# Spreading the narrowing of feed-forward weights over the routed experts and over single operations

## The chip, the cores and the metric

The kernel runs on one core of one Trainium2 chip. The metric is the time of one execution on the device, in microseconds (us). TensorE is called PE, VectorE DVE, ScalarE ACT, GpSimd POOL, and SyncE, which issues most transfers, SP.

## The reference, cut to what matters

```python
def reference(**kwargs):
    attn_out = _attn_ref(q, k, v)              # decayed linear attention, 4 x 8 heads x 768 x 64
    x = tokens_by_512(attn_out)                # 3072 tokens x 512
    x = _moe_ref(x, ...)                       # 8 experts, one per token (argmax): relu(x @ w1[e]) @ w2[e], gated
    return _moe2_ref(x, ...)                   # dense: rms norm, then silu(xn @ w_gate) * (xn @ w_val) @ w_out
```

The first feed-forward layer is routed: each token uses one of 8 experts (512 to 1024 to 512). The second is dense: 512 to 1536, gated, and back to 512. Its three matrices make 36 tiles of 128 x 512.

## The kernel before

The kernel has three stages: attention with the routing (up to about 173 us of the profile), the eight routed experts one after the other (w = 0 to 7, largest first, with 448 down to 368 tokens each), and the dense layer over 8 blocks of 384 tokens, taken in four passes of two blocks each. Only the first pass (p == 0) has to prepare weights; the other three reuse them.

**High and low parts.** The matmuls run on rounded 32-bit floats, so each operand is split in a high part and a rest, and a product is three matmuls. `split_weights` (L178) makes the two parts of a weight tile: ACT copies it to the high part (L179), POOL subtracts (L180). An expert has 8 tiles of 128 x 1024 (64 in all, numbered t = 8 w + f). Activations are split by ACT and DVE: after `up` (12 matmuls, L285) ACT writes `hh` (L291) and DVE `hl` (L292); `down` (12 matmuls, L298) uses `hh` in eight matmuls and `hl` in the last four. In the loop, `up` of tile t comes before `down` of tile t-1.

**Narrowing.** The dense layer's weights arrive as 64-bit numbers. `uconvs_to` (L209) turns a tile into floats: ACT works on the high words twice (L219, L220), DVE takes four operations (L223, L226, L229, L232), and `umove` (L206) then splits the result, one tile late, with ACT (L179) and POOL (L180). Two tiles share one weight slot, and the results pass through two buffers `fu`. The 36 tiles are called u0 to u35.

**Slots and order.** There are 12 weight slots of 128 x 2 x 1024 (`NSLOT`), three raw buffers for arriving tiles (`NRAW`), and each engine works through its own queue in the order in which the program is written. Expert tile t uses slot t % 12, and its conversion is written up to nine steps ahead of its use (`convs_to`, L829 on). Dense tiles take the slots that come free behind the experts, 7 of them narrowed during the last expert (one for each step from t = 57 on), 7 more up to the first two feed-forward slices, and then three in each slice f of the first pass: one whole tile between the two blocks' `gate`s and two whole tiles after the second.

**The dense layer's slice.** `gate` (L740) makes 24 matmuls (L747) for one block and slice, then ACT takes the silu (L754), DVE multiplies (L755), ACT rounds (L756) and DVE subtracts (L757); `project` (L761) makes 9 matmuls with the result (L765). Both blocks write the same two banks `ps[:, 0]` and `ps[:, 1]`. While an expert runs, `settle` normalises the one before it on DVE: squares are added (L326), halved (L334), inverted (L343) and the rows scaled (L347).

Of the kernel before, what the change touches and what calls it, by code (L numbers as in the profile page):

```python
# [103 lines left out]
def fused_kernel(  # L104
# [60 lines left out]
    def wslot(t):  # L165
        return wt[t % NSLOT if t < NWT + NSLOT else t - NWT]

# [16 lines left out]

    state = {"load": 0, "conv": 0, "end": NPRE, "uload": 0, "uconv": 0}

    def loads_to(t):
        while state["load"] < min(t, state["end"]):
            n = state["load"]
            load_expert_weights(raw[n % NRAW], window_expert(n // NF), n % NF)  # L190
            state["load"] += 1

    def convs_to(t):
        while state["conv"] < min(t, state["end"]):
            n = state["conv"]
            loads_to(n + NRAW - 1)
            split_weights(wslot(n), raw[n % NRAW])
            state["conv"] += 1

    def uraw(u):  # L200
        return raw[(NWT + u) % NRAW].bitcast(I32)

    def uloads_to(u):
        while state["uload"] < min(u, NU):
            SP.dma_start(out=uraw(state["uload"]), in_=wm2[state["uload"]].bitcast(I32))
            state["uload"] += 1  # L206

    def umove(j):
        split_weights(wslot(NWT + j // 2), fl_u[j % 2], j % 2)  # L209

    def uconvs_to(n):
        n = min(n, NU)
        while state["uconv"] < n:
            j = state["uconv"]
            uloads_to(j + NRAW)
            v = uraw(j).rearrange("p (c t) -> p c t", t=2)
            lo, hi = v[:, :, 0], v[:, :, 1]
            u, b = fl_u[j % 2], fl_b[0]
            ACT.activation(out=u, in_=hi, func=AF.Abs, scale=2.0 ** -20)  # L219
            ACT.activation(out=u, in_=u, func=AF.Abs, bias=mid)  # L220
            if j:
                umove(j - 1)
# [3 lines left out]
            DVE.scalar_tensor_tensor(  # L226
                out=b, in0=lo, scalar=29, in1=b, op0=ALU.logical_shift_right, op1=ALU.bitwise_or
            )
            DVE.scalar_tensor_tensor(  # L229
                out=b, in0=hi, scalar=-(1 << 30), in1=b, op0=ALU.bitwise_and, op1=ALU.bitwise_or  # L230
            )
            DVE.scalar_tensor_tensor(out=u, in0=u, scalar=127.0, in1=b.bitcast(F32), op0=ALU.is_le, op1=ALU.mult)  # L232
            state["uconv"] += 1
            if j == NU - 1:
                umove(j)

# [179 lines left out]
    with ExitStack() as es:  # L416
# [289 lines left out]
        totals_b()  # L706
        state["end"] = NWT

# [165 lines left out]
    gate(1, 0)  # L874
    uconvs_to(8)
    project(0, 0)
    ex.mean(w, n, 3)
    ex.store(w - 1, CAPS[w - 1], wpos(w - 1), both(w - 1))
    gate(0, 1)
    uconvs_to(9)  # L880
    ex.inverse(0, n // 2)
    project(1, 0)
    gate(1, 1)
    uconvs_to(11)
    ex.inverse(n // 2, n)
    project(0, 1)
    gate(0, 2)
    uconvs_to(12)
    project(1, 1)
    gate(1, 2)  # L890
    uconvs_to(13)
# [3 lines left out]
    uconvs_to(14)  # L895
# [74 lines left out]
    with tc.If(flag > 0):  # L970
# [33 lines left out]
        with ExitStack() as es:  # L1004
            staging(es)
            wc = pool(es, "wcb")
            wt.extend(wc.tile([128, 2, 1024], F32R, name=f"wb{i}") for i in range(NSLOT, NW2))
            state.update(uload=0, uconv=0)
            uconvs_to(NU)
# [57 lines left out]
```

## Time and profile before

| what | us |
|---|---|
| median of 3 runs (lowest, highest) | 1119.85 (1118.16, 1119.85) |
| the profiled execution's own time | 1119.29 |
| its span in the profile | 1117.2 |
| PE busy | 1055.5 (94%) |
| DVE, ACT, POOL busy | 550.9, 381.4, 337.2 |

The span is the time between the first and the last instruction of the program; about 2.1 us of the execution lie outside it. The busy time of PE counts a matmul from its start to its modelled end, and matmuls overlap, so short pauses vanish in it. The routed experts run from about 173 to 490 us, the first pass of the dense layer from about 490 to 655 us, and the other three passes after that.

### The profile page before, as it was taken

How to read it: one execution, taken by the hardware profiler on the slowest of the kernel's cores; microseconds unless marked ns; L12 is line 12 of the kernel's file. 1: busy time of each engine (PE TensorE's matmuls, PEld its weight loads, DVE VectorE, ACT ScalarE, POOL GpSimd, SP SyncE). 2: the span in 40 equal slices, each digit the busy share in tenths (PEclk: the TensorE clock that was granted, in tenths of full speed). 3: DMA queues.
4: the chain of work that ended last, by engine and by line, in shares of the span. 5: the costliest groups of instructions: out<-in, count | busy, mean ns of one | idle time of the engine just before them, and what ended most of it. 6: DMA issues, size and time to landing. Idle time of an engine off the chain costs nothing.

```text
span 1117.2 us, 16379 instructions
## 1 busy us (share of the span) xinstructions
PE 1055.5 (94%) x6393; PEld 982.8 (88%) x6394; DVE 550.9 (49%) x1045; ACT 381.4 (34%) x721; POOL 337.2 (30%) x271
## 2 busy tenths in 40 slices
PE   7788889999999999989899899999999999999995
PEld 6687779989999999978788799999999999999995
DVE  4699963256666676888888831111311112211111
ACT  1344333444444544555555531111311112211111
POOL 3355544556466656332433310000110000200002
PEclk9899989999999999999999999999999999999998
DMA  8999724445446555543343220000210000100001
GB/s 301 229 307 284 204 63 135 123 135 197 155 142 205 182 156 155 171 104 94 114 141 114 85 85 29 1 1 1 64 50 1 1 1 30 57 1 1 1 1 60
DMA packets 47864, 116.74 MB, mean 104 GB/s; under 512 B 12966, under 2 KB 24486, under 8 KB 44962
## 3 DMA queue, kind: packets, MB, share of 16 engines
q1 hardware_dynamic: 39602, 97.05, 28.8%
q0 software_dynamic: 4864, 12.53, 3.2%
q10 hardware_dynamic: 3312, 6.03, 1.6%
q8 instruction: 52, 0.85, 0.3%
q14 instruction: 34, 0.28, 0.1%
HBM read 93.06 MB, written 23.11 MB: 104 GB/s over the span
## 4 chain that ended last, share of the span: by engine, by line
issue 43%; PE 25%; DVE 11%; POOL 3%; DMA 2%; ACT 2%; POOLq 0%; DVEq 0%; SPq 0%; ACTq 0%
PE ps L285 12%; PE ps L298 11%; DVE fb L226 2%; DVE fb L229 2%; POOL out_dram L780 2%; DVE fu L232 1%; DVE fb L223 1%; PE ps L271 1%; DMA out_dram<-ob,perm 1%; DVE a L755 1%; DVE al L757 1%; ACT ah L756 1%; DVE ys L347 1%; PE ps L604 1%; DMA raw<-wm 1%
## 5 line engine op out<-in xcount | busy, mean ns | idle before, releaser
L747 PE MATMUL ps<-zh,w 128*128 128x384 f32 x960 | 255.2, 336 | 2.6 <-DVE hl L292 1.3
L755 DVE TENSOR_TENSOR a<-a,ps 128x384 f32<-128x384 f32 x96 | 52.8, 550 | 320.2 <-PE ps L747 317.7
L180 POOL TENSOR_TENSOR w<-raw,w 128x1024 fp32r<-128x1024 f32 x64 | 154.7, 2426 | 103.0 <-ACT w L179 102.2
L747 PEld LDWEIGHTS ps<-zh,w 128*128 128x128 f32 x960 | 174.6, 188 | 5.7 <-ACT a L754 1.7
L747 PE MATMUL ps<-xh,w 128*128 128x384 f32 x576 | 156.5, 341 | 9.8 <-ACT a L754 7.2
L747 PE MATMUL ps<-zl,w 128*128 128x384 f32 x480 | 161.2, 336 | 0.0
L285 PE MATMUL ps<-xh,w 128*128 128x448 f32 (+7 forms) x512 | 149.6, 353 | 0.1
L765 PE MATMUL ps<-w,ah 128*128 128x512 f32 x564 | 145.5, 393 | 0.2 <-ACT ys L320 0.2
L780 POOL DMA_INDIRECT out_dram<-xw,perm x10 | 9.9, 992 | 423.3 <-ACT xw L778 420.1
L756 ACT ACTIVATE ah<-a 128x384 fp32r<-128x384 f32 x94 | 49.3, 525 | 209.6 <-DVE a L755 209.6
L747 PEld LDWEIGHTS ps<-xh,w 128*128 128x128 f32 x576 | 104.9, 188 | 17.3 <-ACT a L754 11.3
L765 PEld LDWEIGHTS ps<-w,ah 128*128 128x128 f32 x564 | 104.7, 188 | 16.6 <-ACT ys L320 0.6
L754 ACT ACTIVATE a<-ps 128x384 f32<-128x384 f32 x96 | 46.7, 487 | 202.6 <-PE ps L747 202.5
L298 PE MATMUL ps<-hh,w 128*128 128x448 f32 (+7 forms) x512 | 106.6, 350 | 0.0
L285 PEld LDWEIGHTS ps<-xh,w 128*128 128x128 f32 x512 | 95.2, 188 | 3.4
L747 PE MATMUL ps<-xl,w 128*128 128x384 f32 x288 | 96.9, 336 | 0.0
L298 PEld LDWEIGHTS ps<-hh,w 128*128 128x128 f32 x512 | 93.8, 188 | 2.9
L747 PEld LDWEIGHTS ps<-zl,w 128*128 128x128 f32 x480 | 90.1, 188 | 2.3
L285 PE MATMUL ps<-xl,w 128*128 128x448 f32 (+7 forms) x256 | 89.8, 351 | 0.0
L180 POOL TENSOR_TENSOR w<-fu,w 128x512 fp32r<-128x512 f32 x36 | 55.7, 1546 | 111.7 <-ACT w L179 108.2
L765 PE MATMUL ps<-w,al 128*128 128x512 f32 x282 | 80.1, 392 | 0.0
L757 DVE TENSOR_TENSOR al<-a,ah 128x384 fp32r<-128x384 f32 x94 | 52.5, 558 | 55.5 <-ACT ah L756 55.5
(154 smaller groups left out, 1497.9 us busy)
## 6 DMA issues: line engine op xcount, KB each, us to landing
raw<-wmoe SPq DMA_DIRECT2D x64, 512.0 KB, 3.9
qkv<-att SPq DMA_DIRECT2D x22, 1024.0 KB, 8.0
raw<-wm SPq DMA_DIRECT2D x36, 512.0 KB, 3.7
xw<-z SPq DMA_DIRECT2D x8, 768.0 KB, 6.4
xr<-row ACTq DMA_DIRECT2D x23, 256.0 KB, 7.8
z<-ys SPq DMA_DIRECT2D x2, 912.0 KB, 7.6
z<-ys SPq DMA_DIRECT2D x2, 896.0 KB, 4.3
z<-ys SPq DMA_DIRECT2D x2, 864.0 KB
```

Of the source, the lines that this page charges most:

```text
L180: POOL.tensor_tensor(out=dst[:, 1, c], in0=src, in1=f32(dst[:, 0, c]), op=ALU.subtract)
L226: DVE.scalar_tensor_tensor(out=b, in0=lo, scalar=29, in1=b, op0=ALU.logical_shift_right, op1=ALU.bitwise_or)
L229: DVE.scalar_tensor_tensor(out=b, in0=hi, scalar=-(1 << 30), in1=b, op0=ALU.bitwise_and, op1=ALU.bitwise_or)
L285: PE.matmul(p, lhsT=wtile[:, s, k * 128:(k + 1) * 128], rhs=x[w % len(xh)][:, k, 0:n], start=(i == 0), stop=(i == 3 * KB - 1),)
L298: PE.matmul(ps[:, 4 + k, 0:n], lhsT=wtile[:, s, 512 + k * 128:512 + (k + 1) * 128], rhs=h, start=(f == 0 and j == 0), stop=(f == NF - 1 an ...
L747: PE.matmul(ps[:, part, 0:BT], lhsT=w2(f, part, s, k * 128, (k + 1) * 128), rhs=zz[:, k], start=(i == 0), stop=(i == 3 * KB - 1),)
L754: ACT.activation(out=a, in_=ps[:, 0, 0:BT], func=AF.Silu)
L755: DVE.tensor_tensor(out=a, in0=a, in1=ps[:, 1, 0:BT], op=ALU.mult)
L756: ACT.activation(out=ah, in_=a, func=AF.Copy)
L757: DVE.tensor_tensor(out=al, in0=a, in1=f32(ah), op=ALU.subtract)
L765: PE.matmul(ps[:, o_bank[b % 2][t]], lhsT=x[:, t * 128:(t + 1) * 128], rhs=w2(f, 2, s, 0, 512), start=(f == 0 and j == 0), stop=(f == NF2 ...
L780: ins = POOL.indirect_dma_start(out=out[:, :], out_offset=bass.IndirectOffsetOnAxis(ap=pm[:, t0 + t], axis=0), in_=o, in_offset=None, boun ...
```

## The change

The last 28 expert tiles (t = 36 to 63) use only 6 slots (`FEW`), slot t % 6. The other six are free from tile 36 on, and 12 dense tiles are narrowed into them while these experts run: after the expert tiles whose number leaves 1, 3 or 5 modulo 7. One list, `jobs`, now holds expert and dense tiles in the order in which they are loaded and converted, and `work_to` advances it by single steps: an expert tile is one step, a dense tile four (one DVE operation each; the first also has the two ACT operations, and starts by splitting the tile before it). From t = 32 on, half of a step's work is written before `down` and the rest after it, and the conversion of an expert tile now stands three steps ahead of its use. In the first pass the target is 2.5 tiles a slice, and the steps are dealt out to four places in the slice: a quarter after the first `gate`, a third of what is left after the first `project`, and so on. Between the last expert's tile 60 and the second slice nothing is narrowed.

```diff
+NFEW = 36
+FEW = 6
...
     def wslot(t):
-        return wt[t % NSLOT if t < NWT + NSLOT else t - NWT]
+        if t < NFEW:
+            return wt[t % NSLOT]
+        if t < NWT:
+            return wt[t % FEW]
+        i = t - NWT
+        return wt[(i + FEW) % NSLOT if i < NSLOT else i]
...
+    jobs, nu = [], 0
+    for n in range(NWT):
+        jobs.append(("m", n))
+        if n >= NFEW and n % 7 in (1, 3, 5):
+            jobs.append(("u", nu))
+            nu += 1
+    jobs += [("u", j) for j in range(nu, NU)]
...
+        if kind == "m":
+            steps.append(lambda: (split_weights(wslot(n), r), flush()))
+        else:
+            u = fl_u[n % 2]
+            narrow = narrow_steps(r.bitcast(I32), u, flush)
+            last = lambda: after.append(lambda: split_weights(wslot(NWT + n // 2), u, n % 2))
+            steps.extend([*narrow[:3], lambda: (narrow[3](), last())])
...
+    def work_to(t, share=1):
+        t = min(t, state["end"])
+        left = len(steps) + sum(4 if kind == "u" else 1 for kind, _ in jobs[state["work"]:max(t, state["work"])])
+        for _ in range(-(-left // share)):
+            if not steps:
+                next_tile()
+            steps.pop(0)()
...
             ex.up(w, f, n, wslot(t))
+            if t >= NFEW - 4:
+                convs_to(t + 4, 2)
...
-            convs_to(min(t + NSLOT - 3, NPRE + max(0, t - 1) * 3 // 2))
-            if t > NWT - NF:
-                uconvs_to(t - NWT + NF)
+            convs_to(max(t + 4, min(t + NSLOT - 3, NFEW, NPRE + max(0, t - 1) * 3 // 2)))
...
+    def ready(f):
+        return 16 + (f - 2) * 5 // 2
...
             gate(b0, f)
+            if p == 0:
+                uconvs_to(ready(f), 4)
...
             if p == 0:
-                uconvs_to(15 + 3 * (f - 3))
+                uconvs_to(ready(f), 3)
             gate(b1, f)
+            if p == 0:
+                uconvs_to(ready(f), 2)
...
             if p == 0:
-                uconvs_to(17 + 3 * (f - 3))
+                uconvs_to(ready(f))
```

How this moves instructions is best seen on DVE. Line numbers are those of each kernel: L292 is L336 in the changed one, L264 L308, L343 L387, L755 L799, L757 L801, L180 L188, and L223, L226, L229, L232 are L202, L208, L211, L214. First, DVE in steps f = 4 and 5 of expert w = 4 (`xl<-ps` splits the next expert's tokens, RECIPROCAL is `settle`'s). Before:

```order
L292 SCALAR_TENSOR_TENSOR hl_1991<-ps,hh_1989 128x408
L343 RECIPROCAL sq_1996<-sq_1996 128x208
L292 SCALAR_TENSOR_TENSOR hl_1992<-ps,hh_1990 128x408
L264 TENSOR_TENSOR xl_1988<-ps,xh_1987 128x400 x2
L343 RECIPROCAL sq_1996<-sq_1996 128x208
```

Changed:

```order
L336 SCALAR_TENSOR_TENSOR hl_1991<-ps,hh_1989 128x408
L202 TENSOR_SCALAR fb<-raw_69 128x512
L208 SCALAR_TENSOR_TENSOR fb<-raw_69,fb 128x512
L211 SCALAR_TENSOR_TENSOR fb<-raw_69,fb 128x512
L387 RECIPROCAL sq_1996<-sq_1996 128x208
L214 SCALAR_TENSOR_TENSOR fu_72<-fu_72,fb 128x512
L336 SCALAR_TENSOR_TENSOR hl_1992<-ps,hh_1990 128x408
L308 TENSOR_TENSOR xl_1988<-ps,xh_1987 128x400 x2
L387 RECIPROCAL sq_1996<-sq_1996 128x208
```

The four operations of a dense tile now stand between two `hl`, three of them ahead of the reciprocal.

Second, POOL during expert w = 5 (`raw` marks an expert tile, `fu` a dense tile). Before:

```order
L180 TENSOR_TENSOR w_88<-raw_69,w_88 128x1024
L180 TENSOR_TENSOR w_89<-raw_70,w_89 128x1024
L180 TENSOR_TENSOR w_90<-raw_68,w_90 128x1024
L180 TENSOR_TENSOR w_91<-raw_69,w_91 128x1024
L180 TENSOR_TENSOR w_92<-raw_70,w_92 128x1024
```

Changed:

```order
L188 TENSOR_TENSOR w_91<-raw_68,w_91 128x1024
L188 TENSOR_TENSOR w_1969<-fu_71,w_1969 128x512
L188 TENSOR_TENSOR w_92<-raw_69,w_92 128x1024
L188 TENSOR_TENSOR w_87<-raw_68,w_87 128x1024
L188 TENSOR_TENSOR w_1969<-fu_72,w_1969 128x512
```

POOL's subtractions for dense tiles come in between those for expert tiles.

Third, DVE in the first pass, from the multiplication of the second block's `gate` to that of the next slice's first block. Before:

```order
L755 TENSOR_TENSOR a_1979<-a_1979,ps 128x384
L757 TENSOR_TENSOR al_1983<-a_1979,ah_1982 128x384
L223 TENSOR_SCALAR fb<-raw_69 128x512
L226 SCALAR_TENSOR_TENSOR fb<-raw_69,fb 128x512
L229 SCALAR_TENSOR_TENSOR fb<-raw_69,fb 128x512
L232 SCALAR_TENSOR_TENSOR fu_72<-fu_72,fb 128x512
L223 TENSOR_SCALAR fb<-raw_70 128x512
L226 SCALAR_TENSOR_TENSOR fb<-raw_70,fb 128x512
L229 SCALAR_TENSOR_TENSOR fb<-raw_70,fb 128x512
L232 SCALAR_TENSOR_TENSOR fu_71<-fu_71,fb 128x512
L755 TENSOR_TENSOR a_1978<-a_1978,ps 128x384
```

Changed:

```order
L799 TENSOR_TENSOR a_1979<-a_1979,ps 128x384
L801 TENSOR_TENSOR al_1983<-a_1979,ah_1982 128x384
L211 SCALAR_TENSOR_TENSOR fb<-raw_70,fb 128x512
L214 SCALAR_TENSOR_TENSOR fu_72<-fu_72,fb 128x512
L202 TENSOR_SCALAR fb<-raw_68 128x512
L208 SCALAR_TENSOR_TENSOR fb<-raw_68,fb 128x512
L211 SCALAR_TENSOR_TENSOR fb<-raw_68,fb 128x512
L214 SCALAR_TENSOR_TENSOR fu_71<-fu_71,fb 128x512
L799 TENSOR_TENSOR a_1978<-a_1978,ps 128x384
```

Eight narrowing operations stood in this gap before; now it is six in a slice of three tiles and four in a slice of two, and a tile may be cut by a `gate`.

## Rows read from the trace of the kernel before

**Rows 1.** The page's first line.
```profile
span 1117.2 us, 16379 instructions
```

**Rows 2.** Windows: stretch, then its length, each engine's busy time (instructions), PE clock, DMA share, GB/s.
```profile
345.00:452.00 107.00, 107.00 (x607) 105.92 (x606) 69.48 (x71) 48.05 (x79) 66.83 (x33) 1.00 0.53 165
452.00:493.00 41.00, 35.28 (x203) 33.78 (x202) 36.72 (x45) 22.65 (x41) 18.87 (x14) 1.00 0.50 145
493.00:655.00 162.00, 150.64 (x768) 135.25 (x767) 133.56 (x182) 86.04 (x155) 52.68 (x36) 1.00 0.34 107
```

**Rows 3.** PE's waits, 445 to 658 us: line, releaser, us in total, times, longest.
```profile
PE ps L747 <- ACT a L754: 8.5, 10, 1.3
PE ps L298 <- DVE hl L292: 4.4, 3, 2.3
```

**Rows 4.** Timeline of DVE in the second pass: start, duration, instruction, idle before.
```profile
682.45 0.55 DVE L755 TENSOR_TENSOR a<-a,ps 128x384 f32<-128x384 f32 x1 [4.55 <-PE ps L747]
...
738.81 0.56 DVE L755 TENSOR_TENSOR a<-a,ps 128x384 f32<-128x384 f32 x1 [4.60 <-PE ps L747]
```

**Rows 5.** Timeline of DVE: the first block's multiplication in slices 3, 10, and after the pass.
```profile
537.22 0.54 DVE L755 TENSOR_TENSOR a<-a,ps 128x384 f32<-128x384 f32 x1
...
634.09 0.54 DVE L755 TENSOR_TENSOR a<-a,ps 128x384 f32<-128x384 f32 x1
...
657.41 0.55 DVE L755 TENSOR_TENSOR a<-a,ps 128x384 f32<-128x384 f32 x1 [2.02 <-PE ps L747]
```

**Rows 6.** Timeline of PE: last expert's first `up`, two later ones, second dense `gate`.
```profile
445.94 0.33 PE L285 MATMUL ps<-xh,w 128*128 128x368 f32 x1
...
458.12 0.33 PE L285 MATMUL ps<-xh,w 128*128 128x368 f32 x1
...
462.15 0.33 PE L285 MATMUL ps<-xh,w 128*128 128x368 f32 x1
...
491.85 0.34 PE L747 MATMUL ps<-xh,w 128*128 128x384 f32 x1
```

**Rows 7.** Groups by line, 493 to 655 us: busy, mean ns, idle before.
```profile
L180 POOL TENSOR_TENSOR w<-fu,w 128x512 fp32r<-128x512 f32 x30 | 47.2, 1572 | 99.6 <-ACT w L179 96.1 <-PE ps L747 3.5
L232 DVE SCALAR_TENSOR_TENSOR fu<-fu,fb 128x512 f32<-128x512 f32 x30 | 46.8, 1560 | 3.1
L226 DVE SCALAR_TENSOR_TENSOR fb<-raw,fb 128x512 int32<-128x512 int32 x29 | 20.7, 715 | 1.0
L757 DVE TENSOR_TENSOR al<-a,ah 128x384 fp32r<-128x384 f32 x24 | 13.4, 559 | 14.2 <-ACT ah L756 14.2
L755 DVE TENSOR_TENSOR a<-a,ps 128x384 f32<-128x384 f32 x24 | 12.9, 540 | 8.1 <-PE ps L747 5.6 <-ACT a L754 2.6
```

**Rows 8.** Groups by line, POOL's gathers, experts 4 to 6, 345 to 452 us.
```profile
L255 POOL DMA_INDIRECT xw<-xr,ix x10 | 11.0, 1101 | 2.6 <-issue 1.7 <-DMA raw<-wmoe 0.3 <-PE ps L285 0.3
```

**Rows 9.** Timeline of DVE, ACT and PE, expert 4: one late `hl` and its user.
```profile
372.02 0.51 ACT L291 ACTIVATE hh<-ps 128x408 fp32r<-128x408 f32 x1 [1.05 <-PE ps L285]
373.86 0.57 DVE L292 SCALAR_TENSOR_TENSOR hl<-ps,hh 128x408 fp32r<-128x408 f32 x1
377.67 0.90 PE L298 MATMUL ps<-hl,w 128*128 128x408 f32 x4
```

**Rows 10.** Timeline of DVE: a slow dense tile in the last expert, first operation and next `hl`.
```profile
461.24 1.24 DVE L223 TENSOR_SCALAR fb<-raw 128x512 int32<-128x512 int32 x1
...
466.33 0.53 DVE L292 SCALAR_TENSOR_TENSOR hl<-ps,hh 128x368 fp32r<-128x368 f32 x1
```

**Rows 11.** Timeline of DVE: a fast dense tile in the last expert.
```profile
490.66 0.42 DVE L223 TENSOR_SCALAR fb<-raw 128x512 int32<-128x512 int32 x1
491.11 0.69 DVE L226 SCALAR_TENSOR_TENSOR fb<-raw,fb 128x512 int32<-128x512 int32 x1
```

**Rows 12.** Timelines of POOL and DVE, expert 4: three subtractions, and `settle`'s halving beside them.
```profile
349.77 7.10 POOL L180 TENSOR_TENSOR w<-raw,w 128x1024 fp32r<-128x1024 f32 x3
352.15 5.18 DVE L334 TENSOR_TENSOR xl<-sq,xh 128x416 fp32r<-128x416 f32 x1
```

More of the change, by code (lines that the diff above doesn't have):

```diff
@@ L183, in load_expert_weights, with narrow_steps, first @@
         SP.dma_start(out=r, in_=wmoe[bass.ds(e, 1), f].rearrange("o p c -> p (o c)"))
[L185 to L218, printed above, removed]
+    def narrow_steps(v, u, before):
+        v = v.rearrange("p (c t) -> p c t", t=2)
+        lo, hi, b = v[:, :, 0], v[:, :, 1], fl_b[0]
+        def first():
             ACT.activation(out=u, in_=hi, func=AF.Abs, scale=2.0 ** -20)
             ACT.activation(out=u, in_=u, func=AF.Abs, bias=mid)
-            if j:
-                umove(j - 1)
+            before()
             DVE.tensor_scalar(
@@ L225, in uconvs_to @@
             )
-            DVE.scalar_tensor_tensor(
+        return [
+            first,
+            lambda: DVE.scalar_tensor_tensor(
                 out=b, in0=lo, scalar=29, in1=b, op0=ALU.logical_shift_right, op1=ALU.bitwise_or
-            )
-            DVE.scalar_tensor_tensor(
+            ),
+            lambda: DVE.scalar_tensor_tensor(
                 out=b, in0=hi, scalar=-(1 << 30), in1=b, op0=ALU.bitwise_and, op1=ALU.bitwise_or
-            )
-            DVE.scalar_tensor_tensor(out=u, in0=u, scalar=127.0, in1=b.bitcast(F32), op0=ALU.is_le, op1=ALU.mult)
@@ L233, in uconvs_to @@
-            state["uconv"] += 1
-            if j == NU - 1:
-                umove(j)
+            ),
+            lambda: DVE.scalar_tensor_tensor(
+                out=u, in0=u, scalar=127.0, in1=b.bitcast(F32), op0=ALU.is_le, op1=ALU.mult
+            ),
+        ]
+    jobs, nu = [], 0
[4 more added lines that the diff above has]
+            nu += 1
+    assert nu <= 2 * (NSLOT - FEW)
+    jobs += [("u", j) for j in range(nu, NU)]
@@ new lines, in fused_kernel, with loads_to @@
+    job_of = {job: i for i, job in enumerate(jobs)}
+    state = {"load": 0, "work": 0, "end": NPRE}
+    steps, after = [], []
+    def loads_to(t):
+        while state["load"] < min(t, state["end"]):
+            i = state["load"]
+            kind, n = jobs[i]
+            r = raw[i % NRAW]
+            if kind == "m":
+                load_expert_weights(r, window_expert(n // NF), n % NF)
+            else:
+                SP.dma_start(out=r.bitcast(I32), in_=wm2[n].bitcast(I32))
+            state["load"] += 1
@@ new lines, in flush, with next_tile @@
+    def flush():
+        for do in after:
+            do()
+        after.clear()
+    def next_tile():
+        i = state["work"]
+        kind, n = jobs[i]
+        r = raw[i % NRAW]
+        state["work"] += 1
+        loads_to(i + NRAW - (kind == "m"))
+        if kind == "m":
+            steps.append(lambda: (split_weights(wslot(n), r), flush()))
+        else:
+            u = fl_u[n % 2]
+            narrow = narrow_steps(r.bitcast(I32), u, flush)
+            last = lambda: after.append(lambda: split_weights(wslot(NWT + n // 2), u, n % 2))
+            steps.extend([*narrow[:3], lambda: (narrow[3](), last())])
@@ new lines, in work_to, with convs_to, uconvs_to @@
+    def work_to(t, share=1):
[5 more added lines that the diff above has]
+            steps.pop(0)()
+    def convs_to(t, share=1):
+        if t:
+            work_to(job_of["m", min(t, NWT) - 1] + 1, share)
+    def uconvs_to(n, share=1):
+        work_to(job_of["u", min(n, NU) - 1] + 1, share)
+        if n >= NU and not steps:
+            flush()
@@ L706, in fused_kernel @@
         totals_b()
-        state["end"] = NWT
+        state["end"] = len(jobs)
     wb = pool(ctx, "wb")
@@ L874, in fused_kernel @@
     gate(1, 0)
-    uconvs_to(8)
     project(0, 0)
@@ L879, in fused_kernel @@
     gate(0, 1)
-    uconvs_to(9)
+    uconvs_to(13)
     ex.inverse(0, n // 2)
@@ L883, in fused_kernel @@
     gate(1, 1)
-    uconvs_to(11)
+    uconvs_to(14)
     ex.inverse(n // 2, n)
@@ L887, in fused_kernel @@
     gate(0, 2)
-    uconvs_to(12)
+    uconvs_to(15, 2)
     project(1, 1)
+    uconvs_to(15)
     gate(1, 2)
-    uconvs_to(13)
     for k in range(KB):
@@ L894, in fused_kernel @@
     project(0, 2)
-    uconvs_to(14)
+    uconvs_to(16)
+    def ready(f):
+        return 16 + (f - 2) * 5 // 2
     obs = ob[:1]
@@ L1007, in fused_kernel @@
             wt.extend(wc.tile([128, 2, 1024], F32R, name=f"wb{i}") for i in range(NSLOT, NW2))
-            state.update(uload=0, uconv=0)
-            uconvs_to(NU)
+            for j in range(NU):
+                r, u = raw[j % NRAW].bitcast(I32), fl_u[j % 2]
+                SP.dma_start(out=r, in_=wm2[j].bitcast(I32))
+                for step in narrow_steps(r, u, lambda: None):
+                    step()
+                split_weights(wslot(NWT + j // 2), u, j % 2)
             with tc.For_i(0, NT, BT) as t0:
```

## The prediction

> **What bounds the kernel now.** I read the page's first line, then the busy time by windows to find where PE is not full, then PE's waits there, then the timelines. The span is 1117.2 us [rows 1]; the profiled execution took 1119.29 us, 2.09 more, and that lies 0.56 below the median of 1119.85. While experts 4 to 6 run, PE is busy for all 107.00 of 107.00 us; in the last expert it is busy for 35.28 of 41.00, in the first pass for 150.64 of 162.00 [rows 2]. The waits that end most of these pauses are for ACT's silu (8.5 us) and for DVE's `hl` (4.4) [rows 3]. DVE is the busiest engine beside PE there: 36.72 of 41 and 133.56 of 162 us, against 69.48 of 107 with the experts before [rows 2]. The narrowing does it. In the first pass a tile costs DVE 420 + 2 x 715 + 1560 ns = 3.41 us (the third operation taken like the second), 3.6 with the gaps between operations [rows 7, 11].
>
> Busy time hides part of the loss, so I measure the loss by pace. In the second pass, with nothing to narrow, ten multiplications lie 56.36 us apart, nine intervals of 6.26 [rows 4]; a slice, which has two, is 12.52. In the first pass slices 3 to 10 are 96.87 us apart, seven intervals of 13.84 [rows 5]. DVE's queue explains the number: three tiles of 3.6, and for each of two blocks 540 ns, a wait for ACT's rounding (14.2 us over 24) and 559 ns, about 1.5 with some overlap, make 13.8 [rows 7].
>
> A step of `up` and `down` without a pause takes 4.03 us (458.12 to 462.15) [rows 6], which is 0.168 for a matmul of 368 columns and 0.175 for one of 384. From the first matmul of the second block's first `gate` (491.85) to the multiplication after the pass (657.41) there are 165.56 us [rows 5, 6]. They hold that `gate` (24 x 0.175 = 4.2), 23 intervals of 6.26, and two matmuls of a mean, 0.4: 148.6. **Loss in the first pass: 17.0 us.** From the last expert's first `up` (445.94) to 491.85 there are 45.91 us [rows 6]. They hold eight steps of 4.03, the `down` of the expert before (2.1), a `gate` (4.2) and a mean (0.4): 38.9. **Loss in the last expert: 7.0 us.** Together 24.0 us could come back, and hardly more.
>
> **The change, part by part.**
>
> *First pass.* A slice has 2.5 tiles instead of 3. DVE then needs 2.5 x 3.6 + 2 x 1.5 = 12.0 us a slice and PE 12.52, so PE becomes the bound by half a microsecond. Slices of three tiles still need 13.8 on DVE, 1.3 too much, and stand next to slices of two at 10.2. PE can take that lateness: the bank that the multiplication frees is written again 2.06 us (`project`, 6.26 - 4.2) and 2.1 (the first half of a `gate`) after the `gate`'s end, the multiplication normally ends about 1.1 after it (silu and itself), which leaves 3.0. Dealing out single operations also shortens the longest run between two multiplications from eight to six, so the silu, which queues on ACT behind the copies of these tiles, is late less often. In slices 0 to 2 four tiles are left of seven: 4 x 3.6 + 6 x 1.5 = 23.4 of 37.6 us on DVE, which leaves 14 for `settle`. I leave 2 us of the 17.0.
>
> *Last expert.* Two tiles of seven stay (u10, u11): 7.0 x 2/7 = 2.0 us stay.
>
> *Experts 4 to 6.* Ten tiles come in, where PE is full now. This stretch's rows don't show what one costs DVE; I bound it. A tile that meets nothing on POOL takes 0.42 + 3 x 0.69 = 2.5 us [rows 11]. One that met POOL in the last expert took 5.1, from 461.24 to the next `hl` at 466.33 [rows 10]. DVE is busy for 69.5 of 107 us [rows 2]; ten tiles bring it to 94.5, to 103.6 (at 3.41), or to 120.5. PE bears some lateness: an `hl` that could have begun at 372.53, when `hh` was done, began at 373.86, and its user ran at 377.67, so a start at 377.1 would still have been in time: 4.5 us of slack [rows 9]. Up to 111.5 us of DVE work may thus pass unseen, and the high end is 9 us of stall. POOL is busier here (66.83 of 107) than in the last expert (18.87 of 41) [rows 2], so I take 4.5 a tile, nearer the high row: 114.5, **3 us of stall**.
>
> *What else moves.* POOL gets ten subtractions of 1.57 us [rows 7]: 66.8 + 15.7 = 82.5 of 107, hidden, since an expert tile is converted three steps (12.1 us) ahead of its use; a POOL further behind than that would make PE wait for weights. SP has some 33 raw loads in this stretch instead of 23, through the same three buffers; the DMA share of 0.53 [rows 2] may rise to 0.76, and each load is issued as soon as the tile three back is done, so it is hidden; without that cover ACT's copy would wait for a load, and the next `hh` behind it. The lists and gathers queue on SP and POOL behind these and are due four steps later. ACT, busy for 48.05 of 107 [rows 2], has room; a dense tile's copy waits on it for DVE's fourth operation and holds up the next `hh`, whose matmuls come two half steps (4 us) later. The other slot numbers cost nothing, as the slots are free by then.
>
> **Sum:** 1119.3 - 24.0 + 2 + 2 + 3 = 1102.3; I say **1102.5 us**. Low end: no stall in experts 4 to 6 and 1 us less in the first pass, 1098.3, and 1097 with the spread of the runs. High end, at 5.1 a tile: 1119.3 - 24.0 + 4 + 9 = 1108.3.
>
> **A rule to weigh.** In expert 4 one DVE operation on two SBUF tensors, begun at 352.15 beside three of POOL's subtractions, ended at 357.33, 0.46 us after POOL's last one at 356.87 [rows 12]; on a quiet POOL such operations take 0.69 [rows 11]. The engines shut each other out, and a whole run of POOL's can pass first. The Trainium skill (SBUF — State Buffer, section "SBUF: two separate sides") says that POOL and a DVE operation with two SBUF inputs, or in a two-port mode, share one pair of ports as an exclusive lock, held for the whole instruction, and that the loser fully blocks. The trace agrees on the blocking. By that rule the two engines' times simply add up, and the sum would be the first rival's.
>
> **The rivals.**
>
> *The port is full (22%).* POOL's 82.5 us less 11.0 of gathers [rows 8], ten tiles of 3.41 on DVE, and `settle`'s 24 operations of 0.69 make 71.5 + 34.1 + 16.6 = 122 in 107 us. Less the slack of 4.5, 10.7 us of stall, 7.7 more than I booked: 1110. For it: [rows 12]; against it: POOL may fall 12 us behind before PE asks for its weights. This is what the Trainium skill's rule would do here.
>
> *Starving: slower (7%).* POOL's subtractions come in runs (expert tile, dense tile, expert tile), and DVE may wait for the end of a run, 5.18 us in [rows 12]. If that befell one operation of each tile, a tile would cost 5.2 + 1.8 = 7.0, ten bring DVE to 139.5, 28 us of stall after the slack, and 1119.3 - 24.0 + 4 + 28 = 1127. It decides from 6.2 us a tile on (69.5 + 62 - 111.5 = 20), where all that is won is given back. Against it: a dense tile's own subtraction needs DVE's fourth operation first, so POOL's runs break off there.
>
> *DVE still sets the pace (10%).* If slices of three tiles take 13.8 and those of two don't make up for it, four pairs lose 1.3 each: 5 us more, 1107.5.
>
> *Nothing is won (5%).* The pauses move into the experts in full: 1118 to 1122. That the change doesn't do what it says is excluded by the order, where the tiles do move.
>
> **How the numbers follow.** The forecast, at 1097 to 1106, has 56%, port 22, pace 10, nothing 5, slower 7. The range of 1097 to 1112 takes in the first three, 88%, less what I may have mistaken. A measurement of this kernel tells 0.2% (2.2 us) from no change. Faster 0.88, same 0.05, slower 0.07.
>
> **What would show it.** Right: slices 3 to 10 at 12.5 to 12.8 us each, silu waits under 2 us in all, the last expert's loss near 2, and PE waiting for `hl` by a few us between tiles 36 and 60. Wrong: slices over 13; PE waits for `hl` or `ys` of over 10 us there; DVE's narrowing operations there above 1.4 us on the mean; PE waiting for POOL's weights at all.

## The result and the profile after

The change made the kernel slower: 1125.52 us (median of 8 runs, 1121.95 to 1126.14) against 1119.2 (8 runs of the kernel before), ratio 1.0051 with a 95% interval of [1.0042, 1.0059]. The forecast was 1102.5, its range ended at 1112. The profiled execution took 1125.93 us, with a span of 1124.2 us [rows 1].

The windows of the changed kernel over the same stretches as [rows 2] (length, busy time of PE, PE's weight loads, DVE, ACT, POOL, each with its instructions, PE clock, DMA share, GB/s):

```profile
345.00:452.00 107.00, 99.18 (x532) 95.12 (x531) 87.36 (x96) 58.58 (x97) 71.86 (x40) 0.97 0.60 188
452.00:493.00 41.00, 31.66 (x179) 30.63 (x178) 25.56 (x32) 20.54 (x37) 24.22 (x13) 0.93 0.53 174
493.00:655.00 162.00, 158.69 (x839) 149.01 (x838) 114.71 (x163) 79.07 (x140) 47.86 (x35) 1.00 0.30 92
```

The first pass is now nearly full (158.69 of 162 us, before 150.64). The experts are not, where PE had been full: 99.18 of 107. And PE's clock, 1.00 in all three stretches before, is granted at 0.97 and 0.93 on the mean.

The first block's multiplication on DVE in slices 3 and 10 and after the pass, as in [rows 5] (start, duration, instruction):

```profile
544.84 0.55 DVE L799 TENSOR_TENSOR a<-a,ps 128x384 f32<-128x384 f32 x1
...
633.29 0.55 DVE L799 TENSOR_TENSOR a<-a,ps 128x384 f32<-128x384 f32 x1 [1.62 <-PE ps L791]
...
662.13 0.56 DVE L799 TENSOR_TENSOR a<-a,ps 128x384 f32<-128x384 f32 x1 [2.02 <-PE ps L791]
```

Seven slices in 88.45 us are 12.64 each, against 13.84. So the first pass runs at the pace that was forecast. Most of the loss is ahead of it, and PE's waits show its places (first three lines: 445 to 662 us, which answer to [rows 3]; the others: 345 to 465 us):

```profile
PE ps L342 <- ACT hh L335: 7.0, 1, 7.0
PE ps L791 <- ACT a L798: 1.5, 1, 1.5
PE ps L791 <- POOL w L188: 1.4, 2, 1.1
...
PE ps L383 <- DVE xl L378: 4.9, 3, 3.6
PE ps L342 <- DVE hl L336: 1.1, 1, 1.1
```

The silu's 8.5 us are down to 1.5, and the 4.4 us of waits for `hl` in that stretch are gone; one of 1.1 us stands ahead of it, among experts 4 to 6, where PE waited for none before. New are a single wait of 7.0 us for `hh`, 4.9 us for the subtraction that `settle` makes ahead of an expert's mean (L334 before, L378 now), and 1.4 us for weights from POOL in the first pass.

**Where the 7.0 us come from** is a chain through three queues (timelines of POOL, SP, ACT and PE in the last expert; the bracket gives the idle time ahead of an instruction and what ended it):

```profile
476.50 5.34 POOL L780 TENSOR_TENSOR zl<-xw,zh 128x384 fp32r<-128x384 f32 x4
...
481.87 0.64 SPq L774 DMA_DIRECT2D xw<-z  x1
482.71 1.46 SPq L191 DMA_DIRECT2D raw<-wmoe  x2
...
488.50 1.06 ACT L187 ACTIVATE w<-raw 128x1024 fp32r<-128x1024 f32 x1 [11.45 <-DMA raw<-wmoe]
...
489.98 0.46 ACT L335 ACTIVATE hh<-ps 128x368 fp32r<-128x368 f32 x1
...
490.49 2.82 PE L342 MATMUL ps<-hh,w 128*128 128x368 f32 x8 [7.02 <-ACT hh L335]
```

The load of the second block of z (the dense layer's input; L774) overwrites rows that POOL reads until 481.84. SP waits for that, and behind it in SP's queue stand the last two expert tiles. ACT waits 11.45 us for the first of them, `hh` (L335) stands behind that copy on ACT, and PE waits for `hh`. Before the change only dense tiles, which nobody needed soon, stood behind this load.

**Where the mean's wait comes from** (timelines of POOL, DVE and PE in expert 6):

```profile
434.78 2.42 POOL L188 TENSOR_TENSOR w<-raw,w 128x1024 fp32r<-128x1024 f32 x1
437.15 1.29 POOL L188 TENSOR_TENSOR w<-fu,w 128x512 fp32r<-128x512 f32 x1
438.40 2.34 POOL L188 TENSOR_TENSOR w<-raw,w 128x1024 fp32r<-128x1024 f32 x1
...
436.15 5.02 DVE L378 TENSOR_TENSOR xl<-sq,xh 128x400 fp32r<-128x400 f32 x1 [0.81 <-ACT xh L377]
...
441.23 0.70 PE L383 MATMUL ps<-xl,ones 128*128 128x400 f32 x1 [3.57 <-DVE xl L378]
```

A run of three subtractions on POOL, the middle one a dense tile's, lasts from 434.78 to 440.74. The DVE operation begun inside it ends 0.43 us after it. Such runs stood there before too, and made the subtraction as long (5.18 us in [rows 12]), but it ended in time, at 357.33, and PE took its result 0.46 us later without a wait (timeline of PE, kernel before, expert 4; in experts 5 and 6 it was 0.8 and 0.4 us later):

```profile
357.79 0.35 PE L339 MATMUL ps<-xl,ones 128*128 128x416 f32 x1
```

The groups of the dense tiles' four operations, 345 to 452 us (busy, mean ns, idle before), which answer to [rows 7] at the new place:

```profile
L214 DVE SCALAR_TENSOR_TENSOR fu<-fu,fb 128x512 f32<-128x512 f32 x9 | 11.9, 1318 | 0.0
...
L208 DVE SCALAR_TENSOR_TENSOR fb<-raw,fb 128x512 int32<-128x512 int32 x9 | 8.3, 923 | 0.3
...
L211 DVE SCALAR_TENSOR_TENSOR fb<-raw,fb 128x512 int32<-128x512 int32 x9 | 6.3, 699 | 0.3
L202 DVE TENSOR_SCALAR fb<-raw 128x512 int32<-128x512 int32 x9 | 5.3, 584 | 1.2 <-DMA raw<-wm 1.2
```

On the mean they are not slow, 3.5 us a tile (584 + 923 + 699 + 1318 ns). It is single operations that come late.

**Both of the long pauses cost twice,** since PE's granted clock fell behind each. The windows of 4 us around the end of the mean's pause in expert 6:

```profile
440.00:444.00 4.00, 2.77 (x9) 2.77 (x10) 3.93 (x6) 1.54 (x2) 1.10 (x2) 0.50 0.38 146
444.00:448.00 4.00, 4.00 (x18) 4.00 (x17) 2.92 (x3) 1.40 (x3) 2.71 (x2) 0.69 0.64 149
```

0.50 is the lower of PE's two levels, 1.2 GHz. Of 2.77 busy us at 0.50 and 4.00 at 0.69, 1.4 and 1.2 us are lost to it, 2.6 together. Behind the 7.0 us pause eight matmuls took 2.82 us (above) instead of the 1.50 that the same eight take one step later.

### The profile page after: what moved, and what is told of

Same layout as the page of the kernel before. It is cut to its first block, busy times and chain, and to the rows that moved or that the text cites. A ratio compares the mean times of both kernels' runs of the same rounds, so it can differ in the third digit from the quotient of the medians.

```text
span 1124.2 us, 16337 instructions
## 1 busy us (share of the span) xinstructions
PE 1056.3 (94%) x6393; PEld 986.6 (88%) x6394; DVE 536.5 (48%) x1045; ACT 381.2 (34%) x721; POOL 332.5 (30%) x271
## 4 chain that ended last, share of the span: by engine, by line
issue 41%; PE 29%; DVE 7%; ACT 3%; DMA 3%; POOL 3%; POOLq 0%; SPq 0%; DVEq 0%; ACTq 0%
PE ps L329 9%; PE ps L342 9%; PE ps L791 7%; PE ps L809 3%; POOL out_dram L824 2%; ACT w L187 1%; DVE ys L391 1%; DVE fu L214 1%; DMA out_dram<-ob,perm 1%; DMA raw<-wm 1%; DVE fb L208 1%; PE ps L315 1%; POOL w L188 1%; DVE fb L211 1%; PE ps L648 1%
## 5 line engine op out<-in xcount | busy, mean ns | idle before, releaser
L799 DVE TENSOR_TENSOR a<-a,ps 128x384 f32<-128x384 f32 x96 | 53.1, 553 | 333.2 <-PE ps L791 328.5
L188 POOL TENSOR_TENSOR w<-raw,w 128x1024 fp32r<-128x1024 f32 x64 | 155.5, 2436 | 120.7 <-ACT w L187 119.7
L791 PE MATMUL ps<-xh,w 128*128 128x384 f32 x576 | 153.8, 338 | 1.5 <-ACT a L798 1.5
L342 PE MATMUL ps<-hh,w 128*128 128x448 f32 (+7 forms) x512 | 109.5, 356 | 9.1 <-ACT hh L335 7.5
L342 PEld LDWEIGHTS ps<-hh,w 128*128 128x128 f32 x512 | 94.9, 191 | 14.1 <-ACT hh L335 8.1
L188 POOL TENSOR_TENSOR w<-fu,w 128x512 fp32r<-128x512 f32 x36 | 52.9, 1470 | 115.3 <-ACT w L187 113.8
L336 DVE SCALAR_TENSOR_TENSOR hl<-ps,hh 128x448 fp32r<-128x448 f32 (+7 forms) x64 | 37.4, 584 | 89.6 <-ACT hh L335 85.2
```

The costliest lines, as they stand in the source:

```text
L188: POOL.tensor_tensor(out=dst[:, 1, c], in0=src, in1=f32(dst[:, 0, c]), op=ALU.subtract)
L336: DVE.scalar_tensor_tensor(out=hl, in0=p, scalar=0.0, in1=f32(hh), op0=ALU.max, op1=ALU.subtract)
L342: PE.matmul(ps[:, 4 + k, 0:n], lhsT=wtile[:, s, 512 + k * 128:512 + (k + 1) * 128], rhs=h, start=(f == 0 and j == 0), stop=(f == NF - 1 an ...
L791: PE.matmul(ps[:, part, 0:BT], lhsT=w2(f, part, s, k * 128, (k + 1) * 128), rhs=zz[:, k], start=(i == 0), stop=(i == 3 * KB - 1),)
L799: DVE.tensor_tensor(out=a, in0=a, in1=ps[:, 1, 0:BT], op=ALU.mult)
```

## The experiments

The changed kernel is the base of each, if nothing else is said. A ratio compares with the kernel before, measured beside the run. Since PE's pauses add up along the experts, I compare when `hl` of a tile began, against the kernel before; each column is set to 0 at tile 34, ahead of the first dense tile. The last column is the multiplication right after the first pass. Each row is one profiled execution, and what the clock does behind a pause can differ between two of them by nearly 3 us (last section), so smaller differences say little here.

| us later than before | 42 | 50 | 58 | 60 | 63 | after the first pass |
|---|---|---|---|---|---|---|
| the change | 2.2 | 6.4 | 13.2 | 20.3 | 14.8 | 5.5 |
| e1_zload_later | 1.7 | 5.2 | 11.0 | 11.1 | 3.9 | -5.4 |
| e2_copy_later | 0.9 | 2.6 | 8.6 | 14.8 | 9.6 | 0.3 |
| e3_both_later | 0.9 | 3.2 | 10.4 | 10.5 | 3.9 | -5.4 |
| e4_dealt_alone | 0.0 | 0.0 | -1.8 | -1.7 | -1.6 | -2.3 |
| e5_mean_later | 1.7 | 4.2 | 12.6 | 12.5 | 5.3 | -4.0 |
| e8_slots_alone | 0.0 | 0.1 | -1.7 | -5.9 | -8.7 | not read |
| p1_no_pool | 0.0 | 0.1 | 0.2 | -3.3 | -8.8 | -18.0 |
| p2_less_vector | 0.2 | 1.6 | 2.5 | -1.3 | -5.4 | -12.8 |
| e9_eight_tiles | 2.7 | 4.2 | 10.3 | 6.1 | 2.4 | 1.0 |
| e10_light_steps | 0.0 | 0.3 | -1.5 | -2.1 | -8.8 | -21.3 |
| e11_places_alone | 0.1 | 2.3 | 3.2 | 10.1 | 5.0 | -4.3 |

### Two places in the queues

**e1_zload_later**: one load written two steps later.

```diff
                     z_split(0, POOL)
+                elif f == 4:
                     z_block(0, 1)
```

> The load of the second block of z moves from step 2 of the last expert to step 4, so that in SP's queue it no longer stands, waiting for POOL's split of the first block, ahead of expert weights. Theory Q (that queue makes the 7.0 us stall of the last expert, and the half clock behind it costs a few us more): no wait of TensorE over 3 us in the last expert, its pause and half clock gone, 1115 to 1119 us. Theory A (ScalarE's queue: the copy of a dense tile waits for VectorE's fourth operation and holds up relu) and theory L (VectorE and GpSimd have too much work together among the experts): relu is as late as before the edit for other reasons, 1123 to 1126 us.

1116.49 us, ratio 0.9966 [0.9954, 0.9978]. The 7 us wait is gone; PE's waits from 340 to 520 us begin now with

```profile
PE ps L383 <- DVE xl L378: 5.7, 4, 3.5
PE ps L383 <- ACT xh L377: 1.0, 1, 1.0
```

In the table tile 60 comes 9 us earlier, tile 63 11. One load's place cost 9.0 us of the median. Theory Q holds, for the last expert; up to tile 58 only 2.2 us changed.

**e2_copy_later**: a dense tile's copy and subtraction half a step later.

```diff
-            steps.append(lambda: (split_weights(wslot(n), r), flush()))
+            steps.append(lambda: split_weights(wslot(n), r))
...
+            flush()
             convs_to(max(t + 4, min(t + NSLOT - 3, NFEW, NPRE + max(0, t - 1) * 3 // 2)))
```

> A finished dense tile's copy and subtraction are issued half a step later among the experts, behind the second matmuls of the step instead of right behind the next expert tile's copy. Theory A: ScalarE no longer waits 20 us in all for VectorE's fourth operation with relu behind it; experts 4 to 6 lose 4 to 8 us against the kernel before instead of 15; 1114 to 1120 us. Theory L: VectorE itself is late, kept out by GpSimd, so hl comes as late as now, 1123 to 1127 us. Theory Q: the 7 us wait in the last expert stays in any case.

1122.55 us, ratio 1.0029 [1.0016, 1.0043]: 3 us better than the change, short of what A gives. ACT's waits for the fourth operation, 24.5 us in the change from 340 to 500 us, are down to 3.3, and tile 50 is 3.8 us earlier. But the mean's wait stays at 3.6 us, and the wait for `hh` in the last expert at 5.3. A is a part, and the smaller one.

**e3_both_later**: both edits.

> Both edits. Q and A together: 1105 to 1111 us, below the kernel before. Q alone: 1115 to 1119 us. L: 1122 us or more.

1114.91 us, ratio 0.9951 [0.9937, 0.9965]: already below the kernel before, and still above the forecast of Q and A together. Tile 58 is 10.4 us late, so the larger part of the experts' loss was neither.

### Which part of the change wins what

**e4_dealt_alone**: the experts as before, the first pass dealt out, still 3 tiles a slice.

```diff
-NFEW = 36
-FEW = 6
+NFEW = 64
+FEW = 4
...
-        return 16 + (f - 2) * 5 // 2
+        return 17 + 3 * (f - 3)
```

The places of the calls among the experts go back to those of the kernel before, and the targets of the first three slices are set to match.

> Experts as before the change (12 slots, no dense tile among them until the last one), and only the other part of the change: single operations dealt over four points of a slice in the first pass, still 3 tiles a slice where the change has 2.5. If the first pass of the kernel before lost its 17 us to blocks of operations (order), 1106 to 1111 us. If it lost them to the quantity of VectorE's work (3 tiles of about 4 us a slice), the slices keep near 13.8 us, 1117 to 1121 us.

1115.92 us, ratio 0.9963 [0.9948, 0.9978]. The multiplications of slices 3 and 10:

```profile
537.11 0.55 DVE L799 TENSOR_TENSOR a<-a,ps 128x384 f32<-128x384 f32 x1
...
632.83 0.55 DVE L799 TENSOR_TENSOR a<-a,ps 128x384 f32<-128x384 f32 x1
```

Seven slices in 95.72 us, 13.67 each: the pace says quantity. The median gained 4.0 us, a little more than quantity allowed; its profiled execution gained 1.7, and in the table most of that is there at tile 58, ahead of the first pass.

**e7_blocks**: e3_both_later with whole tiles at two places in a slice.

```diff
-            if p == 0:
-                uconvs_to(ready(f), 4)
...
-                uconvs_to(ready(f), 3)
+                uconvs_to(ready(f) - 1)
             gate(b1, f)
-            if p == 0:
-                uconvs_to(ready(f), 2)
```

> The run e3_both_later, with the first pass's tiles given out whole at two points of a slice, as before the change, but still 2.5 tiles a slice. If the number of tiles sets the pace (3 tiles dealt in single operations still ran at 13.8 us a slice), the slices keep 12.6 us and the time is that of e3_both_later within 3 us: 1113 to 1118 us. If single operations matter as well, TensorE waits for silu again, 0.5 to 1 us a slice: 1120 to 1126 us.

1116.05 us, ratio 0.9969 [0.9956, 0.9982], slices of 12.61 us. With 2.5 tiles a slice it makes no more than some 2 us whether they come whole or in single operations.

**e8_slots_alone**: `n % 7 in (1, 3, 5)` becomes `n % 7 in ()`.

> The changed kernel without the 12 dense tiles among the experts (they come behind the last one, so that the first slices of the feed-forward part read slots that do not hold their tiles yet: part of the output is another, and only the experts' stretch is read). It prices the 6 slots and the shorter look-ahead alone. If all of the 14 us that the experts lose are the dense tiles' work, the last expert's last hl comes as early as before, within 1 us, or earlier; if the shorter look-ahead loses time by itself, 2 us or more later.

One run, 1140.68 us, which says nothing of the experts. Their last `hl` began 8.7 us earlier than before, and tile 50 on time. Six slots cost nothing; all that the experts lose comes from the dense tiles among them, and the 8.7 us earlier are about what the 7 tiles of the last expert cost before (7.0 by the prediction's measure).

### What the dense tiles collide with

**e5_mean_later**: e3_both_later with the mean behind the next `up`.

```diff
             ex.up(w, f, n, wslot(t))
+            if w and f == 5:
+                ex.mean(w - 1, CAPS[w - 1], 3)
...
-        elif f == 4:
-            ex.mean(w, n, bank)
-            ex.inverse(0, n // 2)
         elif f == 5:
-            ex.inverse(n // 2, n)
+            ex.inverse(0, n // 2)
         elif f >= 6:
+            if f == 6:
+                ex.inverse(n // 2, n)
```

> Both edits of the run e3_both_later, and the mean of an expert's squares moves half a step later: behind the first matmuls of step 5 instead of the end of step 4. In e3_both_later TensorE still waits 5.9 us for VectorE's subtraction ahead of that mean, 3.6 us of it at once, and its clock is granted at 0.94 and 0.89 in the 40 us behind that. Theory P (pauses, and the half clock that follows a long one, are what is left of the loss among the experts): the waits go and with them the dips, 7 to 9 us in all: 1105 to 1109 us. Theory L (VectorE and GpSimd are too full there): the wait turns up at the next thing that VectorE owes, hl or the split of the next rows, 1112 to 1116 us.

1117.19 us, ratio 0.9984 [0.997, 0.9998]: 2 to 4 us worse than e3_both_later. The wait moved to the next thing that DVE owes, as L has it (PE's waits, 340 to 500 us):

```profile
PE ps L342 <- DVE ys L353: 4.9, 2, 4.3
PE ps L342 <- DVE hl L336: 2.8, 3, 1.2
PE ps L383 <- DVE xl L378: 1.6, 1, 1.6
```

**p1_no_pool** and **p2_less_vector** take away what DVE may be late by: POOL's subtractions of the expert tiles from 36 on, or 24 of DVE's own operations.

```diff
-            steps.append(lambda: split_weights(wslot(n), r))
+            steps.append(
+                lambda: ACT.activation(out=wslot(n)[:, 0], in_=r, func=AF.Copy)
+                if n >= NFEW else split_weights(wslot(n), r)
+            )
```

```diff
+            if n < 12:
+                narrow[1:3] = [lambda: None] * 2
             steps.extend([*narrow[:3], lambda: (narrow[3](), last())])
```

> The run e3_both_later without GpSimd's subtraction for the expert tiles from 36 on (their low half stays that of an older tile, so the output is another). The step e5 spoke for theory L: the wait only moved. L has two forms. Port (VectorE's operations are long because GpSimd's runs keep them out): VectorE's operations of 3 to 6 us in 340 to 480 us shrink to 1.5 us or less, VectorE's busy time there falls from 16 to 13 us or less in 20, and the last expert's last hl comes 5 us or more earlier than in e3_both_later. Quantity (VectorE has too much of its own): its busy time stays over 15 in 20 and hl comes at most 2 us earlier.

> The run e3_both_later without the second and third VectorE operation of each of the 12 dense tiles among the experts (24 operations of about 0.7 us; the output is another). Quantity: some 17 us less of VectorE's time between 340 and 490 us, and the last hl 5 us or more earlier. Port: these operations are a small part; the runs of GpSimd still hold the others up, and hl comes at most 3 us earlier.

One run each: 1099.51 and 1109.98 us. Without POOL's subtractions of these tiles nothing is late, and the subtraction ahead of the mean (L381 in this kernel), which took 5.02 us in the change and 6.54 in e3_both_later, takes 0.58; DVE's busy time over 160 us from 340 on falls from 128.8 (e3_both_later) to 94.9. First the operation in expert 6 of e3_both_later, then the same in p1_no_pool, then a window of that run:

```profile
431.57 6.54 DVE L378 TENSOR_TENSOR xl<-sq,xh 128x400 fp32r<-128x400 f32 x1 [1.52 <-ACT xh L377]
...
428.42 0.58 DVE L381 TENSOR_TENSOR xl<-sq,xh 128x400 fp32r<-128x400 f32 x1 [0.88 <-ACT xh L380]
```

```profile
420.00:440.00 20.00, 20.00 (x119) 19.93 (x118) 12.90 (x20) 12.63 (x20) 3.35 (x3) 1.00 0.78 248
```

But with less work for DVE (109.1 us in the same 160) the last `hl` also came 9.3 us earlier than in e3_both_later, although the subtraction in expert 6 still took 6.33 us and PE still waited 2.4 for it. By the expectations each form of L is borne out, so these two runs do not choose between them; they say that DVE and POOL together are too slow somewhere. Whether in sum or at certain moments, the next two tell.

**e9_eight_tiles**: fewer tiles, at other steps (`n % 7 in (1, 4)`), four more up to slice 2, then `16 + (f - 2) * 8 // 3`.

> Both edits, 8 dense tiles among the experts instead of 12, 8 more in the first three slices instead of 4, and then 8 tiles in 3 slices. Theory L (each dense tile among the experts costs TensorE about 1 us, and in the first pass, up to 8 in 3 slices, nothing): experts 3 to 5 us better than in e3_both_later, the lead at the end of the first pass kept (4 us): 1105 to 1109 us. If the first three slices have no room for four more tiles, this is given back: 1110 to 1114 us.

1118.12 us, ratio 0.9996 [0.9978, 1.0014]. Both halves of the expectation failed: tile 58 is as late with 8 tiles as with 12 in e3_both_later (10.3 and 10.4 us), PE waits 6.6 us for the subtraction ahead of the mean, and the first pass has its waits for silu again (5.2 us). Since the 8 tiles also stand at other steps, this run says only that fewer tiles alone don't help.

**e10_light_steps**: 12 tiles at other steps, the two queue edits, and 8 tiles in 3 slices.

```diff
-        if n >= NFEW and n % 7 in (1, 3, 5):
+        if n >= NFEW - 1 and n % 8 in (3, 5, 7):
...
-        return 16 + (f - 2) * 5 // 2
+        return 16 + (f - 2) * 8 // 3
```

> Both edits, 8 tiles in 3 slices in the first pass, and the 12 dense tiles put at steps 1, 3 and 7 of an expert, where VectorE has one or two operations of its own besides hl, instead of at every second or third step whatever falls there. If what counts is which step is too full: 1105 to 1109 us. If only the sum of the work counts: 1110 to 1113 us, the 4 us of the kept lead alone.

1100.76 us (1098.59 to 1101.32), ratio 0.9832 [0.9818, 0.9845]: faster than both kernels, and better than expected. The tiles now fall on the same three steps of every expert; modulo 7, against steps that go by 8, they wandered through all eight. But these steps are 1, 3 and 5, not 1, 3 and 7 as this expectation and that of e11_places_alone say: a dense tile behind expert tile n of the list is narrowed two steps before step n, and DVE's first operation on one follows the `hl` of tiles 33, 35, 37, 41, 43, 45 and so on. Step 5 holds a half of the inverse and two splits of the next rows, so it is not that the tiles went to steps where DVE has little else to do. The same three windows as above, and the subtraction ahead of the mean:

```profile
345.00:452.00 107.00, 107.00 (x605) 105.73 (x604) 89.18 (x106) 64.87 (x108) 80.76 (x39) 1.00 0.65 202
452.00:493.00 41.00, 40.59 (x237) 39.89 (x236) 27.00 (x35) 22.70 (x43) 23.55 (x15) 1.00 0.53 151
493.00:655.00 162.00, 161.43 (x850) 151.00 (x849) 114.57 (x162) 78.90 (x141) 48.67 (x40) 1.00 0.32 99
```

```profile
431.28 0.58 DVE L378 TENSOR_TENSOR xl<-sq,xh 128x400 fp32r<-128x400 f32 x1
```

DVE and POOL are as busy among the experts as after the change, or more (89.18 and 80.76 us against 87.36 and 71.86), and PE is full at full clock. So they were not too full in sum.

What the places change can be read from the subtraction ahead of the mean, which stands in step 3. In experts 4 and 6 the change narrows a tile in step 2, and the subtraction took 2.44 and 5.02 us; in expert 5 its tiles fall on steps 1, 3 and 5, and it took 0.58. Wherever a run narrows a tile in step 2 of experts 4 to 6 and POOL makes all its subtractions, it took 2.4 to 7.3 us; in p1_no_pool, at the same steps, at most 0.59. With tiles at steps 1, 3 and 5 it took 0.58 in e10_light_steps in all three experts; at the same steps but with the copies where the change has them (e11_places_alone) it was 2.77 in expert 6. (With no dense tile among the experts, in e8_slots_alone, it took 2.7 to 3.3, and PE did not wait.) A tile in step 2 thus lengthens POOL's run of subtractions just where the mean's operand is due. Which other steps do harm by themselves was not tried.

**e6_lead_kept**: e5_mean_later with the 8 tiles in 3 slices.

> The run e5_mean_later, with 8 tiles in 3 slices of the first pass instead of 5 in 2. After the change the lead of the narrowed tiles runs out in slice 14: TensorE waits there for a copy, a subtraction and an activation, and two slices take some 5 us more. If that is for want of lead alone, these 4 to 6 us come back against e5_mean_later; if VectorE cannot give more than 2.5 tiles in 12.5 us, every slice gets longer by 0.2 to 0.6 us and nothing is won (0 to 5 us lost).

1113.8 us, ratio 0.9947 [0.9933, 0.9962], 3.4 us better than e5_mean_later, and slices of 12.57 us against 12.64. The lead was what was lacking at the end, in slices 10 and 11 (the last two; the 14 in the expectation is a slip).

**e11_places_alone** and **e12_places_lead**: the changed kernel with the new condition alone, and with the 8 tiles in 3 slices as well; the queues as in the change.

> The changed kernel with one condition changed: the 12 dense tiles are put at steps 1, 3 and 7 of an expert instead of at every second or third step. Nothing is changed in the queues. If the places are the cause of what experts 4 to 6 lose (theory P2: a step that holds the mean, its halves or the next rows' splits has no room for four operations more), TensorE's waits for hl, hh and the mean in 340 to 460 us go and the clock stays at 1.00 there: about 12 us better than the change, and the 7 us wait in the last expert may stay: 1106 to 1114 us. If the queues are the cause, 1120 to 1126 us.

> The same, and 8 tiles in 3 slices of the first pass. Against e11_places_alone 3 to 4 us better (the lead at the end of the first pass). Against e10_light_steps (1100.8 us), which has the two queue edits as well: equal within 2 us if the queue edits only mend what the wrong places broke; 7 us or more slower if the load of z in SP's queue still holds up the last expert.

1115.47 us, ratio 0.9956 [0.9941, 0.9971], and 1112.03, ratio 0.9934 [0.9918, 0.995]. The places are worth 10.0 us, a little less than expected: among experts 4 to 6, PE still waits 1.5 us for DVE's evacuation of an expert (`ys`) and 1.1 for `hl`, which are gone where the copies stand later as well (e10_light_steps). The wait of 6.8 us for `hh` is still there in e11_places_alone, and 6.9 in e12_places_lead, which is 11.3 us slower than e10_light_steps: the load of z still holds up the last expert. PE's waits of e11_places_alone:

```profile
PE ps L342 <- ACT hh L335: 6.8, 1, 6.8
PE ps L342 <- DVE ys L353: 1.5, 2, 1.1
```

From the change's 1125.5, the places give 10.0, the lead 3.4, and the two queue edits the last 11.3 us, down to 1100.8. (By the ratios, each to the kernel before in its own round, 10.6, 2.5 and 11.4.)

## Why the prediction was wrong

By its own measures (from the last expert's first `up`, 457.80 now, and the first matmul of the second block's first `gate`, 508.59 now):

| loss in us | before | forecast | measured |
|---|---|---|---|
| experts 4 to 6 | 0 | 3 | 12.6 |
| last expert | 7.0 | 2 | 11.9 |
| first pass | 17.0 | 2 | 4.9 |

The first line is 457.80 - 445.94 = 11.86, and 0.78 by which the changed kernel stood earlier when the dense tiles began. The others are 508.59 - 457.80 - 38.9 and 662.13 - 508.59 - 148.6. Together 29.4, 5.4 more than before. Less those 0.8, and with some 2.3 us more from the end of the first pass to the end of the span (462.07 against 459.79, all of it in the last 30 us, and not pursued), they make the 7.0 us by which the span grew.

- **First pass: right in its mechanism, 3 us too good.** With 2.5 tiles a slice PE becomes the bound (12.64, forecast 12.5 to 12.8; silu waits 1.5, forecast under 2). That single operations help the silu is not borne out (e7_blocks). The 3 us are the lead that runs out in slices 10 and 11 (PE waits there for weights and one silu; e6_lead_kept and e12_places_lead win 3.4 us with more lead), which the text did not follow to the end of the pass.
- **Experts 4 to 6: the first of two steps that failed.** The text booked 4.5 us of DVE time for a tile and said that 111.5 us of DVE work may pass unseen in 107, and counted the rest as stall. A tile cost less, 3.5 us by the groups shown above, DVE was busy for 87.4, and PE still stalled. e10_light_steps carries 89.2 without a stall. A sum over a stretch does not bound the stall when single results are due at fixed moments: what stalls PE is the one operation that meets a run on POOL just ahead of its use, and whatever stands behind it. The slack of 4.5 us of one `hl` [rows 9] was taken for that of every result; the mean's was 0.46 us in the same expert. PE's waits in the stretch (4.9 and 1.1 us above, and 1.8 for three others) and the clock's 2.6 make 10.4 of the 12.6; the rest was not pursued.
- **The second: "each load is issued as soon as the tile three back is done, so it is hidden",** and with it the 2 us of the last expert. SP issues in its own order, and the z load ahead waited for POOL. The text had the very consequence ("ACT's copy would wait for a load, and the next `hh` behind it") without looking for what stands on SP's queue there. Of the 11.9 us, the pause is 7.0, two other waits (for `xl` 1.3, for ACT's `ys` 1.0) make 2.3, and the clock behind the pause, at 0.50 and 0.72 in two windows of 4 us, about 1.9. e1_zload_later shows 9.0 us for the load alone.
- **A dense tile's copy holding up `hh`, booked at nothing:** e2_copy_later prices it at 3.0 us, and on top of the other queue edit it is 1.6 (1116.49 to 1114.91).
- **The clock was not in the sum.** In the rows of the stretches before it was 1.00, so each pause was priced once.
- **The signs.** Slices and silu came as under "right". Of those under "wrong", the waits for `hl` and `ys` stayed at 1.7 us and the narrowing operations under 1.4 on the mean; only PE's wait for POOL's weights showed, 1.4 us in the first pass. No sign named the two waits that made the loss.
- **The rivals.** "Starving" gave 1127 with the right place (POOL's runs) and the wrong price (5.2 us for one operation of each tile, which took 3.5 in all); that it comes within 2 us of 1125.5 is luck, since it has neither the load nor the clock. "The port is full" gave 1110; e10_light_steps excludes that it is full. By the Trainium skill (SBUF — State Buffer, section "SBUF: two separate sides") the loser of the port pair blocks for the other's instruction. The trace shows the blocking, but DVE's subtraction, begun inside one POOL instruction, ended only after two more, as above; there the measurement goes further than the page. Without POOL's subtractions it took 0.58 us.
- The 1102.5 that was forecast for the change is near what its parts give with the tiles at other steps, two places in the queues mended and more lead in the first pass (1100.8). That does not confirm the sum: it booked 3 us of stall among experts 4 to 6, and PE waits for nothing there in e10_light_steps.

## What to carry to other kernels

When work is spread into a stretch that is full, do not compare sums of busy time alone. Ask, for each step of the loop, how much slack the user of each result has, and put the work at fixed steps that leave these results alone; a stride that does not divide the loop tries every bad place in turn. For each load that becomes urgent, read what stands ahead of it in its issuing queue and what that waits for. Price a long pause of PE both with and without a slower clock behind it: here it cost up to 2.8 us more.

## What the runs showed of the hardware

The same pause does not always cost the clock. e3_both_later and e7_blocks are the same program up to the first pass, and in both PE waits 3.63 us for the mean in expert 6. The PE timeline of that matmul and a window behind it, first of e3_both_later:

```profile
438.16 0.70 PE L383 MATMUL ps<-xl,ones 128*128 128x400 f32 x1 [3.63 <-DVE xl L378]
...
440.00:444.00 4.00, 4.00 (x14) 4.00 (x13) 3.96 (x4) 1.71 (x3) 2.37 (x1) 0.50 0.47 138
```

and of e7_blocks:

```profile
437.88 0.45 PE L383 MATMUL ps<-xl,ones 128*128 128x400 f32 x1 [3.63 <-DVE xl L378]
...
440.00:444.00 4.00, 4.00 (x27) 3.97 (x26) 4.00 (x6) 2.55 (x5) 3.96 (x2) 1.00 0.55 146
```

In the one the clock fell to 0.50 and 14 matmuls went by in 4 us, in the other it stayed at 1.00 and 27 did. It made 2.8 us by tile 63 (3.9 and 1.1 us later than before, measured like the table). Why it fell in one alone stays open.
